# A fused attention and two mixers on one core: third-pass weights from ScalarE's queue, earlier stores, earlier token mixing, another order of Strassen's first products

## The chip, the cores and the metric

The kernel runs on one core of a Trainium2 chip. The metric is the device time of one execution in microseconds; it is the median of three runs. One further execution was profiled, and all durations come from that one.

## The reference

Float32, batch 2, 768 tokens, 8 heads of 64. The middle stage's and the last stage's weights arrive as float64.

```python
def reference(q, k, v, centroids, ...):
    # cluster attention: a key counts only where its cluster is the query's
    mask = argmax(qn @ cn.T) == argmax(kn @ cn.T)
    scores = where(mask, q @ k.T / sqrt(64), -1e9)
    x = (softmax(scores) @ v)                  # -> (2, 768, 512)
    # mixer 1
    u = x + (x.T @ U @ V).T                    # rank 32 over the 768 tokens
    x = u + maximum(u @ w_ch1, 0) @ w_ch2      # 512 -> 2048 -> 512
    # mixer 2
    u = x + (maximum(x.T @ w_tok1, 0) @ w_tok2).T   # 768 -> 256 -> 768
    return u + maximum(u @ w_ch1, 0) @ w_ch2   # 512 -> 1536 -> 512
```

## The kernel before

Each operand of a matrix product is held as a high and a low part, so that each product is three matmuls (high·high, high·low, low·high). There are three stages on one core.

**Attention** fills the first 239 us or so, and isn't touched.

**Mixer 1's channel mixing** takes the 1536 tokens in three passes of 512 over the 16 blocks of weights, which makes 48 units. A unit is two *half slots*: `hidden(k+1)`, 12 matmuls of 512 columns into one PSUM bank, and `outmm(k)`, 12 matmuls that accumulate into four banks. `hidden_out` turns a hidden bank into the operand of `outmm`: ScalarE takes the Relu (L786), and VectorE then the low part (L787), each from PSUM. The half slots are numbered 0 to 95. The first two passes keep their weights in SBUF; those of the third come back from DRAM (`scr_a`) by `feed`, 32 loads of 512 KB into three buffers. At half slot n, `feed(n)` may issue one load: a unit's first half once `hidden_out` of the unit two ahead of it is written into the program, its second half once the `outmm` two units ahead is. Either load has then three half slots until its first use.

Beside this runs work in the background, a piece each half slot. `conv_rest` turns mixer 2's float64 weights into high and low parts, a *quad* of blocks at a time: a raw load of 1 MB (L535), ScalarE's L96, VectorE's L100, L103, L106 and L109, sums of blocks for Strassen's scheme (step 6), the high parts on ScalarE and GpSimd's low parts (step 7), VectorE's low part (step 7.5), and two stores into `scr_b` of 768 KB and 1 MB (step 8, L617 and L618). A table, `line`, gives each quad a half slot h, and the steps stand at fixed distances from it. `tok(0)`, the token mixing of the first batch, begins at half slot 68 and goes in 20 pieces: 6 of transposes, 6 of the first product and 8 of the second. Behind it, `build_u(0)` makes the operands of Strassen's products out of the result, 18 small operations, three in a half slot, on ScalarE, VectorE and GpSimd.

**Mixer 2's channel mixing** is Strassen's scheme: seven products for each pair of blocks. Six *runs* of 14 steps follow one another. In a step TensorE does six matmuls of 384 columns of a hidden product for the next run (`h_mm`) and six of an output product of this run (`o_mm`). Then `h_out` works the hidden product off, and `o_out` (VectorE, L1150) adds the output product to the result, in this order on VectorE. `CHAIN` lets products alternate between two banks; the bank of the last output product, steps 12 and 13, is the one with which the next run begins. `ORDER` lists the seven products in the order in which both kinds are made; `CHUNKS` and `PLACE` say which of them one load brings and where they lie in `scr_b`. `tok(1)` and the first run's hidden products stand ahead of the runs, `build_u(1)` beside the first two.

SP issues all the DMAs of the second and third stage, in program order: an issue that waits holds all that stand behind it. The loads' and stores' completions are counted on eight semaphores, in turn.

Of the kernel before, what the change touches and what calls it, by code (L numbers as in the profile page):

```python
# [24 lines left out]
def tile_cluster_attention__then__two_mixers(  # L25
# [895 lines left out]
    def rest_of_u():  # L921
# [21 lines left out]
        for i in range(len(ops) + 1):  # L943
# [13 lines left out]
            (wide, 13, 37), (wide, 14, 40), (wide, 15, 43), (mixer, 1, 46), (mixer, 2, 48), (mixer, 3, 50)]  # L957
    line += [(quad, q, h) for q, h in enumerate((54, 59, 62, 65, 69, 72, 75, 79, 82, 85, 89, 92))]
    for n, (f, k, h) in enumerate(line, 6):
        steps = [(h - 4, (3,)), (h - 3, (4, 4.5)), (h - 2, (5, 5.5))]  # L960
        if f is quad:
            steps += [(h - 1, (6,)), (h, (7,)), (h + 1, (7.5,)), (h + 3, (8,))]
        else:
            steps += [(h, (6, 6.5)), (h + 1, (7,))]
        if n > 7:
            steps.append((line[n - 8][2] - 1, (1,)))
        for s, ds in steps:
            for d in ds:
                at(wides, s, (f, k, d, n))
# [6 lines left out]

    ORDER = (1, 5, 6, 3, 7, 2, 4)
    PLACE = (0, 3, 4, 5, 6, 1, 2)
# [5 lines left out]
    FRESH = (True, True, False, False, False, True, False)  # L984

    slot = lambda x, i: x[:, 1536 * i : 1536 * i + 1536].rearrange("p (h c n) -> p h c n", h=2, c=2)
    pos = lambda i: ORDER.index(i)
    base = [slot(u1_, i) for i in range(3)] + [slot(wx_, i) for i in range(2)] + [slot(qk_, 7), slot(vz, 0)]
# [3 lines left out]
    def build_u(b):  # L992

        B = {(i, j): x2[b][:, 2 * i : 2 * i + 2, ts(j, HS)] for i in range(2) for j in range(2)}
        o = {i: ops_u[b][pos(i)] for i in ORDER}
        hi = lambda i: o[i][:, 0]
        lo = lambda i: o[i][:, 1]

        def flat(i, x):
            return [lambda: rnd(act, hi(i), x), lambda: sub(pool, lo(i), x, f32(hi(i)))]  # L1000

        t = [fz[:, 768 * i : 768 * i + 768].rearrange("p (c n) -> p c n", c=2) for i in range(2)]

        def cut(i, x, eng=pool):
            return [lambda: rnd(act, hi(i), x), lambda: sub(eng, lo(i), x, f32(hi(i)))]

        def add(o, x, y, op):
            return [lambda: dve.tensor_tensor(out=o, in0=x, in1=y, op=op)]  # L1008

        return (flat(1, B[0, 0]) + add(t[0], B[0, 0], B[0, 1], ALU.subtract) + cut(5, t[0], dve) + add(t[1], B[1, 1], t[0], ALU.add)  # L1010
                + cut(6, t[1], dve) + add(t[0], B[1, 0], t[1], ALU.subtract) + flat(3, B[1, 1])
                + add(t[1], B[1, 1], B[0, 1], ALU.subtract) + cut(7, t[1]) + flat(2, B[1, 0]) + cut(4, t[0], dve))

    gfree = [x.rearrange("p (h n) -> p h n", h=2) for x in (qk_[:, ts(i, 2 * HS)] for i in range(14))]
    gs = {}
    tmps, w1b = [], []
# [22 lines left out]
    def load1(n):  # L1039
        if n < len(seq1):  # L1040
            b, pr, c = seq1[n]
            s, m = CHUNKS[c]
            x = w1b[n % len(w1b)][:, 0 : 512 * m]
            sp.dma_start(f32(x), scr2[pr, 0, :, 512 * PLACE[s] : 512 * (PLACE[s] + m)])
            for i in range(m):
                at1[b, pr, s + i] = x[:, ts(i, 512)].rearrange("p (h n) -> p h n", h=2), n, i == m - 1

    def load2(n):
        if n < len(seq2):
            b, k, c = seq2[n]  # L1050
            s, m = CHUNKS[c]
            x = w2b[n % len(w2b)][:, 0 : 1024 * m].rearrange("p (r n) -> p r n", r=2)
            sp.dma_start(f32(x), scr2[2 * k : 2 * k + 2, 1, :, 512 * PLACE[s] : 512 * (PLACE[s] + m)].rearrange("r p n -> p r n"))
            for i in range(m):
                at2[b, k, s + i] = x[:, :, ts(i, 512)].rearrange("p r (h n) -> p r h n", h=2), n, i == m - 1

# [3 lines left out]
    def h_mm(b, pr, s):  # L1060
        w, n, ends = at1[b, pr, s]
        u = ops_u[b][s]
        o, on = ps[:, HB[pr % 2][CHAIN[s]], 0:HS], dict(skip_group_check=not FRESH[s])
        for c in range(2):
            cs = ts(c, P)
            mm(o, w[:, 0, cs], u[:, 0, c, :], c == 0 and FRESH[s], False, **on)
            mm(o, w[:, 0, cs], u[:, 1, c, :], False, False, **on)
            mm(o, w[:, 1, cs], u[:, 0, c, :], False, c == 1, **on)
        if ends:
            load1(n + len(w1b))  # L1070

    def h_out(b, pr, s):
# [17 lines left out]

        if s == 0:
            held_[1] = tmp()
            act.copy(held_[1], x)
        elif s == 1:
            held_[3] = tmp()
            act.copy(held_[3], x)
        elif s == 2:
            held_[0] = tmp()
            act.copy(held_[0], x)
        elif s == 3:  # L1100
            dve.tensor_tensor(out=held_[0], in0=x, in1=held_[0], op=ALU.add)
            act.activation(held_[0], held_[0], AF.Relu)
        elif s == 4:
            new(3, 7)
            held_[7] = tmp()
            dve.tensor_tensor(out=held_[3], in0=x, in1=held_[3], op=ALU.add)
            top(3, held_[3])
            relu_less(held_[7], held_[3], held_[0], ALU.subtract)
            cut(7, held_[7])
        elif s == 5:  # L1110
            new(1, 5, 6)
            held_[5], held_[6] = tmp(), tmp()
            dve.tensor_tensor(out=held_[1], in0=x, in1=held_[1], op=ALU.add)
            top(1, held_[1])
            relu_less(held_[5], held_[1], held_[0], ALU.subtract)
            cut(5, held_[5])
            relu_less(held_[6], held_[3], held_[5], ALU.add)
            rnd(act, hi(6), held_[6])
            low(1, held_[1])
            low(3, held_[3])  # L1120
        else:
            new(2, 4)
            top(2, x)
            relu_less(held_[0], x, held_[6], ALU.subtract)
            sub(pool, lo(6), held_[6], f32(hi(6)))
            cut(4, held_[0])
            low(2, x)

    def o_mm(b, k, s, j):
        w, n, ends = at2[b, k, s]  # L1130
        o, on = ps[:, OB2[j][CHAIN[s]], 0:HS], dict(skip_group_check=not FRESH[s])
# [28 lines left out]
    bg = [rest_of_u(), conv_rest()]  # L1160
    while done < 68:
        for t in bg:
# [34 lines left out]
    for r, (b, k) in enumerate(runs):  # L1197
# [3 lines left out]
        for i in range(14):  # L1201
# [6 lines left out]
            if nxt:  # L1208
                for x in {6: (), 7: (6, 7)}.get(i, (i,)):
                    h_out(nxt[0], 2 * nxt[1] + x // 7, x % 7)  # L1210
            o_out(b, k, s_, j)
            send(2 if nxt else 0)
# [45 lines left out]
```

## Time and profile before

| | us |
|---|---|
| three runs | 758.09, 756.66, 754.59 |
| median | 756.66 |
| the profiled execution | 757.82 |
| its span | 756.0 |
| TensorE matmuls, busy | 730.5 (97%) |
| VectorE, busy | 565.1 (75%) |
| ScalarE, busy | 371.9 (49%) |
| GpSimd, busy | 221.9 (29%) |
| DMA, moved | 165.36 MB, 219 GB/s on average |

Busy is what an engine's instructions cover of the span. A matmul that runs at half the clock counts as busy too, so that a busy TensorE may still lose time. All times in the rows are from the start of the span.

### The profile page before, as it was taken

To read this page: it belongs to the slowest core of one execution; us is meant where nothing else is said; L and a number is where in the kernel's file an instruction comes from. 1 tells how busy PE (TensorE), PEld (TensorE's weight loads), DVE (VectorE), ACT (ScalarE), POOL (GpSimd) and SP (SyncE) were. 2 spreads that over 40 slices of the span, in tenths; PEclk is the share of its full clock that TensorE was granted. 3 is DMA by queue.
4 is the path that set the end of the run, shared out by engine and by line. 5 is a ranking of instruction groups with operands and counts; after the bars stand their busy time and mean duration, and the time that the engine had idled before them with its cause. 6 is when DMAs were issued, how large, how long until landed. Compare 5 with 4: busy or idle time off the path is not lost.

```text
span 756.0 us, 11118 instructions
## 1 busy us (share of the span) xinstructions
PE 730.5 (97%) x4046; PEld 606.9 (80%) x4046; DVE 565.1 (75%) x829; ACT 371.9 (49%) x660; POOL 221.9 (29%) x181
## 2 busy tenths in 40 slices
PE   7899999999999999999999899999699999899998
PEld 6676777776776888888888677888589999899997
DVE  7778898877875658867878886789855687675674
ACT  7678778777785533333334334333243435333330
POOL 6233153133111123341332212122521425242230
PEclk9999999999999999999999999999899999999999
DMA  6797588765231446763536799989745877587734
GB/s 180 188 226 206 148 218 217 198 186 122 66 102 67 156 178 231 270 222 134 201 114 234 300 410 359 394 309 413 250 151 171 337 258 248 173 292 266 260 132 160
DMA packets 54134, 165.36 MB, mean 219 GB/s; under 512 B 7456, under 2 KB 16544, under 8 KB 50496
## 3 DMA queue, kind: packets, MB, share of 16 engines
q1 hardware_dynamic: 53648, 163.83, 65.4%
q10 hardware_dynamic: 432, 0.82, 0.3%
q8 instruction: 32, 0.52, 0.3%
q14 instruction: 22, 0.18, 0.1%
HBM read 103.61 MB, written 41.94 MB: 193 GB/s over the span
## 4 chain that ended last, share of the span: by engine, by line
PE 85%; DVE 8%; DMA 5%; issue 1%; ACT 1%; POOL 0%; SPq 0%; POOLq 0%; DVEq 0%; ACTq 0%
PE ps L73 74%; PE ps L323 9%; DMA qk<-scr_a 2%; DMA scr_b<-qk 1%; DMA tt<-scr_b 1%; DVE mid L1058 1%; PE ps L386 1%; PE ps L343 1%; DVE qk L1058 1%; DVE fz L1008 1%; DVE c__78 L109 1%; PE ps L409 0%; DMA qk<-p 0%; DVE fz L85 0%; DVE ug L85 0%
## 5 line engine op out<-in xcount | busy, mean ns | idle before, releaser
L73 PE MATMUL ps<-ug,qk 128*128 128x512 f32 x576 | 143.7, 402 | 10.4 <-DVE ug L787 5.7
L73 PEld LDWEIGHTS ps<-ug,qk 128*128 128x128 f32 x576 | 111.0, 194 | 34.8 <-DVE ug L787 6.4
L73 PE MATMUL ps<-qk 112*128 112x384 f32 (+2 forms) x480 | 114.7, 366 | 3.5 <-DMA qk<-p 2.0
L73 PE MATMUL ps<-qk,tt 128*128 128x384 f32 (+1 forms) x528 | 107.9, 344 | 4.4 <-DVE xn L1150 4.1
L301 DVE TENSOR_REDUCE nm<-ps 128x1 f32<-128x768 f32 x96 | 91.2, 955 | 27.9 <-PE ps L73 26.6
L73 PEld LDWEIGHTS ps<-qk,tt 128*128 128x128 f32 x528 | 94.6, 189 | 7.9 <-DVE xn L1150 6.4
L306 ACT ACTIVATE p<-ps,nm 128x768 f32<-128x768 f32 x96 | 86.2, 900 | 22.5 <-DVE nm L301 21.8
L323 PEld LDWEIGHTS ps<-ident,p 128*128 128x128 f32 x576 | 68.4, 141 | 32.6 <-issue 26.9
L323 PE MATMUL ps<-ident,p 128*128 128x128 f32 x576 | 91.0, 278 | 0.5 <-DVE pt L328 0.3
L73 PEld LDWEIGHTS ps<-qk 112*128 112x128 f32 (+1 forms) x480 | 80.7, 190 | 12.4 <-issue 4.4
L786 ACT ACTIVATE ug<-ps 128x512 fp32r<-128x512 f32 x48 | 28.6, 596 | 114.7 <-PE ps L73 109.8
L1150 DVE TENSOR_TENSOR xn<-ps,xn 128x384 f32<-128x384 f32 x84 | 46.0, 553 | 39.0 <-PE ps L73 38.8
L787 DVE SCALAR_TENSOR_TENSOR ug<-ps,ug 128x512 fp32r<-128x512 f32 x48 | 33.1, 689 | 54.1 <-ACT ug L786 54.0
L85 POOL TENSOR_TENSOR qk<-mid,qk 128x384 fp32r<-128x384 f32 x36 | 41.5, 1161 | 107.8 <-ACT qk L78 94.5
L73 PE MATMUL ps<-pt,vr 128*64 128x384 f32 x384 | 72.1, 498 | 0.0
L85 POOL TENSOR_TENSOR qk<-c__78,qk 128x512 fp32r<-128x512 f32 (+1 forms) x26 | 33.9, 1323 | 128.1 <-ACT qk L78 111.8
L330 ACT COPY pt<-ps 128x512 f32<-128x512 f32 x96 | 55.7, 586 | 25.1 <-PE ps L323 24.0
L73 PEld LDWEIGHTS ps<-pt,vr 128*64 128x64 f32 x384 | 23.5, 136 | 25.8 <-issue 25.4
L106 DVE SCALAR_TENSOR_TENSOR c__78<-c__77,c__78 128x1024 int32<-128x1024 int32 (+2 forms) x32 | 42.9, 1341 | 0.2
L85 POOL TENSOR_TENSOR am<-am,amx 128x384 f32<-128x384 f32 (+1 forms) x13 | 10.9, 841 | 109.1 <-DVE amx L214 74.6
L109 DVE SCALAR_TENSOR_TENSOR c__78<-c__77,c__78 128x1024 int32<-128x1024 int32 (+2 forms) x32 | 41.6, 1299 | 1.0
L96 ACT ACTIVATE c__78<-c__77 128x1024 f32<-128x1024 f32 (+2 forms) x32 | 35.5, 1110 | 12.5 <-DMA c__77<-in_wb_dram 6.0
(216 smaller groups left out, 1215.2 us busy)
## 6 DMA issues: line engine op xcount, KB each, us to landing
tt<-scr_b SPq DMA_DIRECT2D x18, 1024.0 KB, 6.3
c__77<-in_wa_dram SPq DMA_DIRECT2D x16, 1024.0 KB, 4.9
qk<-scr_a SPq DMA_DIRECT2D x32, 512.0 KB, 12.8
ring<-scr_b SPq DMA_DIRECT2D x30, 512.0 KB, 4.9
c__77<-in_wb_dram SPq DMA_DIRECT2D x12, 1024.0 KB, 7.7
scr_b<-qk SPq DMA_DIRECT2D x12, 1024.0 KB, 13.0
scr_a<-qk SPq DMA_DIRECT2D x16, 512.0 KB, 2.8
scr_a<-wx SPq DMA_DIRECT2D x12, 512.0 KB, 3.5
```

Of the source, the lines that this page charges most:

```text
L73: pe.matmul(o, lhsT=l, rhs=r, start=start, stop=stop, **kw)
L85: eng.tensor_tensor(out=o, in0=a, in1=b, op=ALU.subtract)
L96: act.activation(dst, hi.bitcast(F32), AF.Abs)
L106: dve.scalar_tensor_tensor(out=d, in0=lo, scalar=29, in1=d, op0=ALU.logical_shift_right, op1=ALU.bitwise_or)
L109: dve.scalar_tensor_tensor(out=d, in0=hi, scalar=-0x40000000, in1=d, op0=ALU.bitwise_and, op1=ALU.bitwise_or)
L301: dve.tensor_reduce(out=nm[:, n % 4 : n % 4 + 1], in_=ps[:, b0 : b0 + 2, 0:HS], axis=AX.XY, op=ALU.max, negate=True)
L306: act.activation(p32[n % NP32].rearrange("p (j k) -> p j k", j=2), ps[:, b0 : b0 + 2, 0:HS], AF.Exp, bias=nm[:, n % 4 : n % 4 + 1], accum_ ...
L323: pe.transpose(ps[:, tb[j], ts(i, P)], p32[n % NP32][:, ts(c, P)], ident)
L330: act.copy(o, ps[:, tb[j], :])
L786: act.activation(gh, o, AF.Relu)
L787: dve.scalar_tensor_tensor(out=gl, in0=o, scalar=0.0, in1=f32(gh), op0=ALU.max, op1=ALU.subtract)
L1150: dve.tensor_tensor(out=o, in0=ps[:, OB2[j][CHAIN[s]], 0:HS], in1=o, op=ALU.add)
```

## The change

Four edits, here with the lines that the argument needs. `feed` issues its loads on ScalarE's queue in place of SP's. The quads come up to two half slots earlier from the fifth on, and each is stored two half slots behind its h in place of three. `tok(0)` begins at half slot 66 in place of 68, and with it all that follows it. Strassen's hidden products get an order of their own, `HORDER`; products 1 and 3 are now finished early, and the cuts of products 4 and 7 are put off to the first step of the next pair.

```diff
-                sp.dma_start(f32(weights(u)[:, i, :, :]).rearrange("p h n -> p (h n)"), scr[f, i])
+                act.dma_start(f32(weights(u)[:, i, :, :]).rearrange("p h n -> p (h n)"), scr[f, i])
...
-    line += [(quad, q, h) for q, h in enumerate((54, 59, 62, 65, 69, 72, 75, 79, 82, 85, 89, 92))]
+    line += [(quad, q, h) for q, h in enumerate((54, 59, 62, 65, 68, 71, 75, 78, 81, 84, 87, 90))]
-            steps += [(h - 1, (6,)), (h, (7,)), (h + 1, (7.5,)), (h + 3, (8,))]
+            steps += [(h - 1, (6,)), (h, (7,)), (h + 1, (7.5,)), (h + 2, (8,))]
...
-    ORDER = (1, 5, 6, 3, 7, 2, 4)
-    CHUNKS = ((0, 1), (1, 2), (3, 2), (5, 2))
+    HORDER, ORDER = (1, 2, 6, 5, 7, 3, 4), (1, 5, 6, 3, 7, 2, 4)
+    HCHUNKS, CHUNKS = ((1, 2), (6, 5), (7, 3), (4,)), ((1,), (5, 6), (3, 7), (2, 4))
...
+    def flush():
+        while behind:
+            behind.pop(0)()
...
         if s == 0:
+            flush()
             held_[1] = tmp()
             act.copy(held_[1], x)
         elif s == 1:
-            held_[3] = tmp()
-            act.copy(held_[3], x)
+            new(1)
+            dve.tensor_tensor(out=held_[1], in0=x, in1=held_[1], op=ALU.add)
+            top(1, held_[1])
+            low(1, held_[1])
...
         elif s == 3:
+            held_[3] = tmp()
+            act.copy(held_[3], x)
+        elif s == 4:
+            new(3)
+            dve.tensor_tensor(out=held_[3], in0=x, in1=held_[3], op=ALU.add)
+            top(3, held_[3])
+            low(3, held_[3])
+        elif s == 5:
+            new(5, 6)
+            held_[5], held_[6] = tmp(), tmp()
             dve.tensor_tensor(out=held_[0], in0=x, in1=held_[0], op=ALU.add)
             act.activation(held_[0], held_[0], AF.Relu)
...
-            new(1, 5, 6)
-            held_[5], held_[6] = tmp(), tmp()
-            dve.tensor_tensor(out=held_[1], in0=x, in1=held_[1], op=ALU.add)
-            top(1, held_[1])
             relu_less(held_[5], held_[1], held_[0], ALU.subtract)
             cut(5, held_[5])
             relu_less(held_[6], held_[3], held_[5], ALU.add)
-            rnd(act, hi(6), held_[6])
-            low(1, held_[1])
-            low(3, held_[3])
+            cut(6, held_[6])
         else:
-            new(2, 4)
+            new(2, 4, 7)
             top(2, x)
-            relu_less(held_[0], x, held_[6], ALU.subtract)
-            sub(pool, lo(6), held_[6], f32(hi(6)))
-            cut(4, held_[0])
             low(2, x)
+            relu_less(held_[1], x, held_[6], ALU.subtract)
+            relu_less(held_[5], held_[3], held_[0], ALU.subtract)
+            behind.extend([lambda h=held_[5], c=cut: c(7, h), lambda h=held_[1], c=cut: c(4, h)])
...
-    while done < 68:
+    while done < 66:
```

**First place: where the third pass begins.** These are rows of SP's queue before. `c__77` is the raw weights' buffer, `qk` and `vz` hold the weights' buffers and the converted operands.

```order
L535 DMA c__77<-in_wb_dram 128x2x512
L766 DMA qk<-scr_a 128x1024
L535 DMA c__77<-in_wb_dram 128x2x512
L766 DMA qk<-scr_a 128x1024
L617 DMA scr_b<-qk 128x1536
L618 DMA scr_b<-qk 128x2048
L766 DMA qk<-scr_a 128x1024 x2
L535 DMA c__77<-in_wb_dram 128x2x512
L766 DMA qk<-scr_a 128x1024
```

A load of weights (L766) stands behind raw loads and stores there. These are ScalarE's rows of the changed kernel at the same place; the Relu is L786, and L879 is a copy of `tok(0)`.

```order
L786 ACTIVATE ug<-ps 128x512
L766 DMA qk<-scr_a 128x1024
L879 CAST wx<-ps 128x512
L766 DMA qk<-scr_a 128x1024
L879 CAST wx<-ps 128x512
L96 ACTIVATE c__78<-c__77 128x1024
L786 ACTIVATE ug<-ps 128x512
L766 DMA qk<-scr_a 128x1024
```

The loads have left SP's queue, where only L535, L617 and L618 remain, and stand among ScalarE's own work.

**Second place: VectorE late in the third pass.** These are the rows between two low parts of the hidden bank (L787) before; `fz` is scratch, L1008 a sum of `build_u(0)`, L85 a low part or a difference.

```order
L787 SCALAR_TENSOR_TENSOR ug<-ps,ug 128x512
L85 TENSOR_TENSOR qk<-fz,qk 128x4x256
L106 SCALAR_TENSOR_TENSOR c__78<-c__77,c__78 128x1024
L109 SCALAR_TENSOR_TENSOR c__78<-c__77,c__78 128x1024
L85 TENSOR_TENSOR u_2310<-fz,u_2310 128x768
L1008 TENSOR_TENSOR fz<-xn,fz 128x768
L85 TENSOR_TENSOR fz<-c__78 128x256
L85 TENSOR_TENSOR fz<-c__78,fz 128x256 x2
L607 SCALAR_TENSOR_TENSOR fz<-c__78 128x256
L1008 TENSOR_TENSOR fz<-xn 128x768
L787 SCALAR_TENSOR_TENSOR ug<-ps,ug 128x512
```

These are the rows between the same two low parts in the changed kernel, where the sums of `build_u(0)` are L1003.

```order
L787 SCALAR_TENSOR_TENSOR ug<-ps,ug 128x512
L85 TENSOR_TENSOR qk<-fz,qk 128x4x256
L106 SCALAR_TENSOR_TENSOR c__78<-c__77,c__78 128x1024
L109 SCALAR_TENSOR_TENSOR c__78<-c__77,c__78 128x1024
L85 TENSOR_TENSOR u_2310<-fz,u_2310 128x768
L1003 TENSOR_TENSOR fz<-xn,fz 128x768
L85 TENSOR_TENSOR fz<-c__78 128x256
L85 TENSOR_TENSOR fz<-c__78,fz 128x256 x2
L607 SCALAR_TENSOR_TENSOR fz<-c__78 128x256
L85 TENSOR_TENSOR wx<-fz,wx 128x768
L1003 TENSOR_TENSOR fz<-xn 128x768
L787 SCALAR_TENSOR_TENSOR ug<-ps,ug 128x512
```

Between these two low parts stands the same work with one more difference, `wx<-fz,wx`, which stood ahead of the first of them before. What moved is what stands behind: two hidden units' low parts in place of one follow the last sums.

**Third place: VectorE at the end of a run.** These are its rows before, at steps 12 and 13, where L1113 works off the bank of step 12's hidden product, L1058 are the sums with a Relu that follow, and L1150 adds step 12's output product.

```order
L1113 TENSOR_TENSOR mid<-ps,mid 128x384
L1058 SCALAR_TENSOR_TENSOR mid<-mid,fz 128x384
L1058 SCALAR_TENSOR_TENSOR mid<-fz,mid 128x384
L1058 SCALAR_TENSOR_TENSOR qk<-mid,qk 128x384
L1058 SCALAR_TENSOR_TENSOR qk<-fz,qk 128x384
L1150 TENSOR_TENSOR xn<-ps,xn 128x384
```

These are the rows of the changed kernel there, with L1118 for L1113 and L1153 for L1150.

```order
L1118 TENSOR_TENSOR mid<-ps,mid 128x384
L1058 SCALAR_TENSOR_TENSOR mid<-mid 128x384 x2
L1153 TENSOR_TENSOR xn<-ps,xn 128x384
```

Two of the five instructions ahead of the output's sum have moved, to steps 1 and 4 of the pair.

## Rows read from the trace of the kernel before

**Rows 1.** The page, part 4: shares of the chain that ended last.

```profile
PE 85%; DVE 8%; DMA 5%; issue 1%; ACT 1%; POOL 0%; SPq 0%; POOLq 0%; DVEq 0%; ACTq 0%
```

**Rows 2.** TensorE's waits over the span: us in total, times, longest.

```profile
PE ps L73 <- DVE ug L787: 5.7, 1, 5.7
PE ps L73 <- DVE xn L1150: 4.1, 4, 2.5
...
PE ps L73 <- DMA qk<-scr_a: 2.1, 2, 2.0
```

**Rows 3.** TensorE's timeline: start, duration, instructions.

```profile
423.87 2.88 PE L73 MATMUL ps<-ug,wx 128*128 128x512 f32 x12
426.59 2.88 PE L73 MATMUL ps<-ug,qk 128*128 128x512 f32 x12
...
463.80 2.88 PE L73 MATMUL ps<-ug,qk 128*128 128x512 f32 x12
...
467.88 2.88 PE L73 MATMUL ps<-ug,qk 128*128 128x512 f32 x12
```

**Rows 4.** Stretches: us, busy of PE, PEld, DVE, ACT, POOL, PEclk, DMA, GB/s.

```profile
429.32:432.02 2.70, 0.16 (x1) 0.03 (x1) 1.76 (x6) 1.05 (x2) 1.44 (x2) 0.96 1.02 419
432.02:439.05 7.03, 7.03 (x25) 5.65 (x26) 5.39 (x6) 1.50 (x3) 0.00 (x0) 0.77 1.02 418
...
454.81:459.23 4.42, 4.42 (x12) 3.42 (x13) 3.84 (x4) 2.53 (x5) 2.43 (x2) 0.61 1.01 386
```

**Rows 5.** Stretches at the end of the third pass, columns as in group 4.

```profile
514.77:547.42 32.65, 26.92 (x109) 21.63 (x109) 29.64 (x31) 12.32 (x18) 15.34 (x8) 0.90 0.83 318
533.80:540.05 6.25, 0.52 (x4) 0.10 (x2) 6.18 (x9) 2.26 (x4) 2.86 (x2) 0.80 0.51 206
540.05:547.42 7.37, 7.37 (x23) 5.92 (x24) 5.30 (x6) 2.24 (x4) 4.90 (x2) 0.70 0.75 251
```

**Rows 6.** Stretches of the third stage, columns as in group 4.

```profile
547.42:556.39 8.97, 8.46 (x55) 7.46 (x53) 4.68 (x9) 5.13 (x10) 0.00 (x0) 1.00 0.70 261
...
646.79:650.54 3.75, 3.75 (x12) 3.75 (x13) 2.76 (x5) 0.89 (x2) 1.00 (x1) 0.54 0.56 231
```

**Rows 7.** The issue of a third-pass load at 420.4 us: KB, us to landing.

```profile
qk<-scr_a SPq DMA_DIRECT2D x1, 512.0 KB, 11.5
```

**Rows 8.** The chain that ended last, near 440 us: start, duration, what.

```profile
438.01 1.24 DVE c__78 L109
...
439.77 14.90 DMA qk<-scr_a
```

**Rows 9.** DMA from 415 to 540 us; KB each, median us to landing.

```profile
DMA packets 9672, 43.88 MB, mean 351 GB/s; under 512 B 960, under 2 KB 960, under 8 KB 8384
...
qk<-scr_a SPq DMA_DIRECT2D x31, 512.0 KB, 12.9
scr_b<-qk SPq DMA_DIRECT2D x10, 1024.0 KB, 13.2
```

**Rows 10.** DMA queues from 2 to 6 us (q1 SP's, q10 ScalarE's): packets, MB, share.

```profile
q1 hardware_dynamic: 253, 0.66, 54.2%
q10 hardware_dynamic: 259, 0.53, 37.7%
```

**Rows 11.** The page, part 6: the quickest transfer of half a megabyte, us to landing.

```profile
scr_a<-qk SPq DMA_DIRECT2D x16, 512.0 KB, 2.8
```

**Rows 12.** ScalarE's timeline near 530 us: start, duration, instruction.

```profile
529.46 0.58 ACT L786 ACTIVATE ug<-ps 128x512 fp32r<-128x512 f32 x1
```

**Rows 13.** VectorE's timeline from 530 to 540 us, columns as in group 12.

```profile
530.84 2.75 DVE L109 SCALAR_TENSOR_TENSOR c__78<-c__77,c__78 128x1024 int32<-128x1024 int32 x1
...
539.30 0.69 DVE L787 SCALAR_TENSOR_TENSOR ug<-ps,ug 128x512 fp32r<-128x512 f32 x1
```

**Rows 14.** VectorE's timeline at the last change of runs, columns as in group 12.

```profile
733.24 0.56 DVE L1113 TENSOR_TENSOR mid<-ps,mid 128x384 f32<-128x384 f32 x1 [0.39 <-PE ps L73]
...
736.78 0.54 DVE L1150 TENSOR_TENSOR xn<-ps,xn 128x384 f32<-128x384 f32 x1
```

More of the change, by code (lines that the diff above doesn't have):

```diff
@@ L995, in build_u, with cut @@
         o = {i: ops_u[b][pos(i)] for i in ORDER}
[L996 to L1000, printed above, removed]
         t = [fz[:, 768 * i : 768 * i + 768].rearrange("p (c n) -> p c n", c=2) for i in range(2)]
-        def cut(i, x, eng=pool):
-            return [lambda: rnd(act, hi(i), x), lambda: sub(eng, lo(i), x, f32(hi(i)))]
+        def cut(i, x, eng):
+            hi, lo = o[i][:, 0], o[i][:, 1]
+            return [lambda: rnd(act, hi, x), lambda: sub(eng, lo, x, f32(hi))]
         def add(o, x, y, op):
             return [lambda: dve.tensor_tensor(out=o, in0=x, in1=y, op=op)]
-        return (flat(1, B[0, 0]) + add(t[0], B[0, 0], B[0, 1], ALU.subtract) + cut(5, t[0], dve) + add(t[1], B[1, 1], t[0], ALU.add)
-                + cut(6, t[1], dve) + add(t[0], B[1, 0], t[1], ALU.subtract) + flat(3, B[1, 1])
-                + add(t[1], B[1, 1], B[0, 1], ALU.subtract) + cut(7, t[1]) + flat(2, B[1, 0]) + cut(4, t[0], dve))
+        early, last = cut(4, t[1], dve), []
+        if b == 0:
+            early, last = last, early
+        return (cut(1, B[0, 0], pool) + cut(2, B[1, 0], pool) + add(t[0], B[0, 0], B[0, 1], ALU.subtract)
+                + add(t[1], B[1, 1], t[0], ALU.add) + cut(6, t[1], dve) + add(t[1], B[1, 0], t[1], ALU.subtract) + early
+                + cut(5, t[0], dve) + add(t[0], B[1, 1], B[0, 1], ALU.subtract) + cut(7, t[0], pool) + cut(3, B[1, 1], pool) + last)
     gfree = [x.rearrange("p (h n) -> p h n", h=2) for x in (qk_[:, ts(i, 2 * HS)] for i in range(14))]
-    gs = {}
+    gs, behind = {}, []
     tmps, w1b = [], []
@@ L1041, in load1 @@
             b, pr, c = seq1[n]
-            s, m = CHUNKS[c]
+            ch = HCHUNKS[c]
+            m, s0 = len(ch), min(STORED.index(i) for i in ch)
             x = w1b[n % len(w1b)][:, 0 : 512 * m]
-            sp.dma_start(f32(x), scr2[pr, 0, :, 512 * PLACE[s] : 512 * (PLACE[s] + m)])
-            for i in range(m):
-                at1[b, pr, s + i] = x[:, ts(i, 512)].rearrange("p (h n) -> p h n", h=2), n, i == m - 1
+            sp.dma_start(f32(x), scr2[pr, 0, :, 512 * s0 : 512 * (s0 + m)])
+            for i in ch:
+                at1[b, pr, i] = x[:, ts(STORED.index(i) - s0, 512)].rearrange("p (h n) -> p h n", h=2), n, i == ch[-1]
     def load2(n):
@@ L1050, in load2 @@
             b, k, c = seq2[n]
-            s, m = CHUNKS[c]
+            ch = CHUNKS[c]
+            m, s0 = len(ch), min(STORED.index(i) for i in ch)
             x = w2b[n % len(w2b)][:, 0 : 1024 * m].rearrange("p (r n) -> p r n", r=2)
-            sp.dma_start(f32(x), scr2[2 * k : 2 * k + 2, 1, :, 512 * PLACE[s] : 512 * (PLACE[s] + m)].rearrange("r p n -> p r n"))
-            for i in range(m):
-                at2[b, k, s + i] = x[:, :, ts(i, 512)].rearrange("p r (h n) -> p r h n", h=2), n, i == m - 1
+            sp.dma_start(f32(x), scr2[2 * k : 2 * k + 2, 1, :, 512 * s0 : 512 * (s0 + m)].rearrange("r p n -> p r n"))
+            for i in ch:
+                at2[b, k, i] = x[:, :, ts(STORED.index(i) - s0, 512)].rearrange("p r (h n) -> p r h n", h=2), n, i == ch[-1]
     def relu_less(o, x, y, op):
@@ L1060, in h_mm @@
     def h_mm(b, pr, s):
-        w, n, ends = at1[b, pr, s]
+        w, n, ends = at1[b, pr, HORDER[s]]
         u = ops_u[b][s]
-        o, on = ps[:, HB[pr % 2][CHAIN[s]], 0:HS], dict(skip_group_check=not FRESH[s])
+        o, on = ps[:, HB[pr % 2][CHAIN[s]], 0:HS], dict(skip_group_check=not HFRESH[s])
         for c in range(2):
             cs = ts(c, P)
-            mm(o, w[:, 0, cs], u[:, 0, c, :], c == 0 and FRESH[s], False, **on)
+            mm(o, w[:, 0, cs], u[:, 0, c, :], c == 0 and HFRESH[s], False, **on)
             mm(o, w[:, 0, cs], u[:, 1, c, :], False, False, **on)
@@ L1210, in tile_cluster_attention__then__two_mixers @@
                     h_out(nxt[0], 2 * nxt[1] + x // 7, x % 7)
+            if not nxt:
+                flush()
             o_out(b, k, s_, j)
```

16 lines of the change are left out of this document (4 added, 12 removed).

## Prediction

> **What bounds the kernel now.** I first read the chain that ended last: 85% of it is TensorE, 8% VectorE, 5% DMA [rows 1]. So the end comes sooner only where TensorE stops waiting or runs faster; no matmul is removed by this change. I then listed TensorE's waits [rows 2]. Three belong to stages that the change touches: 5.7 us once for the low part of a hidden bank (VectorE, L787), 4.1 us in four pieces for an output sum (L1150), 2.1 us for loads of weights. Last I cut the span into stretches around each, with the granted clock beside the busy time. There the reader is to see that a wait costs twice. Twelve matmuls take 2.72 us from start to start [rows 3], so 24 take 5.44; behind the wait that ends at 432.02 the same 24 take 7.03 at a mean clock of 0.77, and behind that at 454.81 twelve take 4.42 at 0.61 [rows 4]. So the engine goes down towards its lower level (1.2 of 2.4 GHz) after it stood still.
>
> The losses, each with its clock:
>
> - **A**, 429.32 to 432.02: the next matmuls start 2.70 us late (the 0.16 busy in it is the end of those before), and 7.03 − 5.44 = 1.59. Sum 4.3.
> - **C**, before 454.81: 2.0 idle [rows 2], and 4.42 − 2.72 = 1.70. Sum 3.7.
> - **E**, 533.80 to 540.05: 6.25 − 0.52 = 5.73 idle, and 7.37 − 5.44 = 1.93 [rows 5]. Sum 7.7.
> - **Changes of runs** in the third stage: 4.1 idle [rows 2]; and behind the longest, 646.79 to 650.54, twelve matmuls of 384 columns take 3.75 us [rows 6] where 2.72 · 384/512 = 2.04 is due, which is 1.7. Sum 5.8.
>
> **The loads on ScalarE's queue (A and C).** Both waits are for loads that came late. That of 420.4 us took 11.5 to land [rows 7], at 431.9, just as TensorE started again. That of C stood on SP behind a raw load that waited for VectorE's L109 (done at 439.25), was issued at 439.77 and took 14.90 [rows 8]. The median load of this stage takes 12.9 us, and the stores in the same queue 13.2 [rows 9], while the DMA engines are full (a share of 1.02 at 418 GB/s [rows 4]). Half a megabyte at 418 GB/s is 1.25 us of that; the rest is standing in line.
>
> On a queue of its own a load needn't stand behind 1.75 MB of stores. Where two queues had work at the same time, at the start of the kernel, they moved 253 and 259 packets, 0.66 and 0.53 MB [rows 10]: about half each. At half of 418 GB/s a load takes 2.5 us, two in a row 5; the quickest transfer of that size lands in 2.8 [rows 11], 1.5 more than its 1.25. So I estimate 4 to 6.5 us to landing. What is there in time? ScalarE issues a unit's first half only behind the Relu of the unit two ahead, three half slots before its use: 3 · 2.72 = 8.2 us, less about 1 for the Relu (0.58 [rows 12]) and the issue, so 7.2. With a piece of token mixing's products in each half slot, which then takes 463.80 to 467.88 = 4.08 [rows 3], it is 11. So I take A and C as gone, −4.3 and −3.7; the bounds are all of it and nothing. The margin in half slots without token mixing is thin.
>
> The 32 issues stand among ScalarE's own work now; ScalarE is busy 12.3 of 32.7 us in the densest stretch [rows 5], where the time to issue hides. What is queued behind an issue that waits (for the semaphore of the eighth DMA before it, often a store) is the next Relu, and behind that VectorE's L787 and `outmm`. The Relu is wanted only two half slots later, 5.4 us, of which Relu and low part need 1.3: some 4 us of cover.
>
> The Trainium skill speaks against this edit. Its page "DMA: Bandwidth & Descriptors", section "Issuing engines are not separate DMA queues", says that DMAs started by several engines run on the same 16 DMA engines and interleave, and that starting them on several saves only the sequencer's time to issue. By that rule alone A and C stay, and the sum would be 754.0. The same page's section "Queues, rings and completion order" says that each DMA engine takes turns between the queues, packet by packet; the trace agrees with that one by its 253 and 259 packets.
>
> **Earlier stores, earlier token mixing.** They remove nothing. The bytes stay (43.88 MB from 415 to 540 us, 351 GB/s on average [rows 9]); a quad's stores come a half slot sooner or more, and some raw loads too, so the line of waiting bytes near 430 us rather grows. That costs nothing as long as the loads have their own turn; if they haven't, it is rival 3. `tok(0)`'s matmuls only change places with half slots that had none. I set both at 0.
>
> **E stays.** ScalarE had the high part ready at 529.46 + 0.58; VectorE made the low part only at 539.30 [rows 12, 13]. VectorE was busy 29.64 of 32.65 us [rows 5], partly because its instructions are stretched where GpSimd works: L109 takes 2.75 us at 530.84 [rows 13] and 1.24 at 438.01 [rows 8]. In the changed order the work between these two low parts is the same and one difference more (about 1 us), which stood just ahead before. The two half slots won behind `build_u(0)` lie behind the stall and can't shorten it. What A and C give back doesn't make it longer either, since VectorE's line of work is paced by the half slots until 514 us. So 0, with bounds −7.7 (rival 2) and +1.
>
> **Changes of runs.** The bank of step 12 is that of the next run's step 0. VectorE's sum for it stood behind L1113 and four more instructions: from 733.24 to 736.78 + 0.54 is 4.1 us [rows 14]. At the last change of runs three groups of six matmuls lie between, 3.06 us, at the others four; so TensorE waits by about 1 there, and elsewhere where `build_u(1)` and GpSimd slow VectorE. Now three instructions stand ahead of it, an add and two sums (0.56 each, as L1113), but between them a Relu on ScalarE that VectorE waits for (at most 0.58, as the wider one [rows 12]). So 3 · 0.56 + 0.58 + 0.54 = 2.8 us, and some 0.1 to 0.2 for handing over: just under 3.06. I take the 5.8 as gone. Bounds: nothing of it, or all.
>
> The new order's costs: at step 1 of each pair VectorE has an add and a low part more (1.1 us). During the runs a step of 2.04 us has room for it; but beside `tok(1)`, 547.42 to 556.39, where TensorE stands for 0.5 already [rows 6], half of it may show: +0.5, bounds 0 and 1.1. The two cuts that `flush` puts ahead of the copy at the next pair's first step are two ScalarE instructions, 1.1 us by the Relu's row, and with the copy 1.6, inside a step of 2.04: nothing, with 0.4 us of cover.
>
> **What else.** `build_u(1)` still puts GpSimd beside VectorE at the first changes of runs, whose longest wait of 2.5 [rows 2] with its clock (4.2 in all) could partly stay: I take 1.0, bounds 0 and 4.2. ScalarE's issues that wait, and a load that lands a little late: 0.5, bounds 0 and 2.
>
> **Sum**, against the profiled execution: 757.8 − 4.3 − 3.7 − 5.8 + 0.5 + 1.0 + 0.5 = 746.0. The median of the runs lies 1.2 under that execution (756.66 against 757.82), so 744.8; I say **745**. The forecast's own range is 742 (none of the additions at all) to 750 (what else at 5 us in place of 1.5, and the 1.1).
>
> **The rivals.**
>
> 1. *The loads come no sooner.* A line of bytes in front of full engines is as long whoever issues, if the load is served in the order of issue: A and C stay, 745 + 8 = 753. The Trainium skill's rule on issuing engines, above, says as much. For it: the engines are full, and the total is unchanged. Against it: the weights need 0.5 MB per half slot of 2.72 us, 193 GB/s, which is less than half of 418, and the two queues at the start shared evenly.
> 2. *E goes too.* If the light half slots let VectorE catch up sooner than I see: 745 − 7.7 = 737. Against it: the same instructions in the same order, at the second place above.
> 3. *Slower: ScalarE issues too late.* SP could issue a load as soon as its buffer was free, up to five half slots ahead; ScalarE can only behind a Relu, three ahead. If a load still takes the 12.9 us of now, the half slots of the full stretch (415 to 459 us, some 12) last (12.9 + 1)/3 = 4.6 in place of 2.72, 23 us more, of which 8 are there already. Half of the other 15, since the line of stores gets shorter while TensorE waits, is 7.5 on a kernel that keeps its other gains: 745 + 8 + 7.5 = 761. It decides from the point where a load takes over 7.2 us from issue to landing in half slots without token mixing. For it: nearly every load takes longer than that now. Against it: half of the packets would do for 6.5.
> 4. *Strassen's new order opens waits.* `flush` and the round trip to the Relu have covers of 0.4 and 0.1 us. If VectorE or ScalarE is later than that in each run, the 5.8 aren't saved: 751, and up to 756 with a lower clock behind each of the waits.
>
> **How the numbers follow.** The forecast has 0.55, rival 1 0.10, rival 2 0.11, rival 3 0.10, rival 4 0.14. 0.5% of 756.7 is 3.8 us, about what a measurement of this kernel can tell from no change: faster is below 752.9, slower above 760.4. The forecast and rival 2 are faster (0.66), of rival 4 two thirds (0.10), of rival 1 less than half (0.04): 0.80. Slower is rival 3 but for a little: 0.09. The rest is 0.11. For 8 in 10 the range goes from the upper half of rival 2 to rival 4's end, 738 to 756, which leaves out about 0.06 below and 0.10 above.
>
> **What would show it.** Right: no wait of TensorE for a load from 415 to 460 us, and loads on ScalarE's queue that land in under 8 us; one wait of some 6 us for L787 near 530; no wait over 0.5 us for an output sum, save at the first changes of runs. Wrong in the loads: landing 10 us or more after the issue, TensorE waiting for one after another, a clock under 0.9 over the whole stretch. Wrong in E: no wait for L787. Wrong in the third stage: TensorE waiting for VectorE's sums at other steps than a run's first, or for ScalarE's copies at step 7.

## The result

The changed kernel takes 749.25 us at the median (748.31 to 749.93, 4 runs) against 755.96 of the kernel before (4 runs): a ratio of 0.9912, 95% interval 0.9886 to 0.9939. It is faster, by 6.7 us where 11 were forecast; the time lies inside the range of 738 to 756, near the upper end of the forecast's own. The profiled execution took 749.86 us, 8.0 less than that of before.

TensorE's waits over the span, in the changed kernel (us in total, times, longest):

```profile
PE ps L73 <- DVE ug L787: 6.2, 2, 5.2
PE ps L73 <- DVE xn L1153: 2.1, 4, 1.2
...
PE ps L73 <- ACT mid L1098: 0.8, 1, 0.8
PE ps L73 <- DMA tt<-scr_b: 0.8, 1, 0.8
PE ps L73 <- issue: 0.7, 1, 0.7
```

Beside [rows 2] the reader sees: no wait for a load of the third pass is left; the long wait for L787 stays (5.2 us in place of 5.7), and a second one of 1.0 has come; the waits for output sums are halved, not gone; two waits of 0.8 us stand in the third stage, a new one for ScalarE's copy of a hidden bank (L1098, L1093 before) and one for a load (0.2 before); and one of 0.7, at 431.30 us, has no releaser that the trace names ("issue").

The stretches between the same matmuls in the two traces, by TensorE's timeline: the third pass from its twelve matmuls `ps<-u,tt` (404.83 before, 405.54 after) to the first `ps<-u,ring` (547.42, 541.52) went from 142.6 to 136.0 us, −6.6. From there to the first output product (583.70, 577.68) 36.3 and 36.2. The runs, from there to the last matmul's end (752.59, 744.03), 168.9 and 166.4, −2.5. What lies ahead of all this, untouched, took 0.7 more in this execution. These three stretches are used below: *third pass* and *runs* are meant in this sense.

### The profile page after: what moved, and what is told of

Read it like the earlier page. It is cut to its first block, busy times and chain, and to the rows that moved or that the text cites. A ratio compares the mean times of both kernels' runs of the same rounds, so it can differ in the third digit from the quotient of the medians.

```text
span 747.6 us, 11096 instructions
## 1 busy us (share of the span) xinstructions
PE 728.4 (97%) x4046; PEld 604.8 (81%) x4046; DVE 557.6 (75%) x829; ACT 370.5 (50%) x660; POOL 215.1 (29%) x181
## 4 chain that ended last, share of the span: by engine, by line
PE 81%; DVE 10%; DMA 3%; ACT 2%; issue 2%; POOL 1%; SPq 0%; ACTq 0%; DVEq 0%; POOLq 0%
PE ps L73 70%; PE ps L323 9%; DVE mid L1058 1%; DVE fz L85 1%; DVE qk L1058 1%; DMA pt<-in_qT_dram 1%; DVE qk L85 1%; DMA tt<-scr_b 1%; DVE xn L1153 1%; PE ps L343 1%; PE ps L386 1%; DVE c__78 L106 1%; DMA scr_b<-qk 1%; DVE ug L787 1%; PE ps L409 1%
## 5 line engine op out<-in xcount | busy, mean ns | idle before, releaser
L73 PE MATMUL ps<-ug,qk 128*128 128x512 f32 x576 | 140.5, 396 | 6.9 <-DVE ug L787 6.2
L73 PEld LDWEIGHTS ps<-ug,qk 128*128 128x128 f32 x576 | 108.8, 190 | 30.2 <-DVE ug L787 7.0
L786 ACT ACTIVATE ug<-ps 128x512 fp32r<-128x512 f32 x48 | 28.6, 596 | 108.7 <-PE ps L73 103.8
L787 DVE SCALAR_TENSOR_TENSOR ug<-ps,ug 128x512 fp32r<-128x512 f32 x48 | 33.0, 688 | 50.4 <-ACT ug L786 50.3
L85 POOL TENSOR_TENSOR qk<-c__78,qk 128x512 fp32r<-128x512 f32 (+1 forms) x26 | 34.4, 1342 | 120.1 <-ACT qk L78 78.2
L1153 DVE TENSOR_TENSOR xn<-ps,xn 128x384 f32<-128x384 f32 x84 | 46.0, 553 | 27.3 <-PE ps L73 27.1
L85 POOL TENSOR_TENSOR qk<-mid,qk 128x384 fp32r<-128x384 f32 x35 | 35.1, 1020 | 106.6 <-ACT qk L78 103.4
L106 DVE SCALAR_TENSOR_TENSOR c__78<-c__77,c__78 128x1024 int32<-128x1024 int32 (+2 forms) x32 | 42.8, 1337 | 0.2
L85 POOL TENSOR_TENSOR am<-am,amx 128x384 f32<-128x384 f32 (+1 forms) x13 | 10.9, 842 | 109.8 <-DVE amx L214 75.4
L73 PE MATMUL ps<-ug,wx 128*128 128x512 f32 (+1 forms) x180 | 41.9, 379 | 0.0
```

Source lines behind the costliest of these rows:

```text
L73: pe.matmul(o, lhsT=l, rhs=r, start=start, stop=stop, **kw)
L85: eng.tensor_tensor(out=o, in0=a, in1=b, op=ALU.subtract)
L106: dve.scalar_tensor_tensor(out=d, in0=lo, scalar=29, in1=d, op0=ALU.logical_shift_right, op1=ALU.bitwise_or)
L786: act.activation(gh, o, AF.Relu)
L787: dve.scalar_tensor_tensor(out=gl, in0=o, scalar=0.0, in1=f32(gh), op0=ALU.max, op1=ALU.subtract)
L1153: dve.tensor_tensor(out=o, in0=ps[:, OB2[j][CHAIN[s]], 0:HS], in1=o, op=ALU.add)
```

## The experiments

**Each edit alone, and the changed kernel without the queue.** The first four kernels split the change along its edits. First the loads alone (e1):

```diff
-                sp.dma_start(f32(weights(u)[:, i, :, :])...
+                act.dma_start(f32(weights(u)[:, i, :, :])...
```

> The kernel before with one edit: the third pass's loads are issued on ScalarE's queue. Theory: both waits for loads and their low clock go (4.3 and 3.7 us), the stall for L787 near 534 us stays at 5 to 7 us, the third stage is as before: about 748 us, 8 less than before. Rival: the loads only come in time because the quads' stores and token mixing also moved; then this edit alone gives less than 4 us, and TensorE still waits for a load near 430 or 453 us.

Measured: ratio 0.9984 (0.9971 to 0.9997), 755.58 us beside 756.45. The rival has it: some 1.2 us, and TensorE still waits for loads, 0.73, 0.83 and 0.79 us at 426.74, 430.61 and 443.94. Why, ScalarE's timeline of this kernel shows (rows with ACTq are DMA issues; in brackets idle time and what ended it):

```profile
423.41 0.96 ACTq L766 DMA_DIRECT2D qk<-scr_a  x2
427.46 0.94 ACT L78 ACTIVATE qk<-c__78 128x256 fp32r<-128x256 f32 x2 [3.47 <-DMA scr_b<-qk]
431.30 1.06 ACT L78 ACTIVATE qk<-fz 128x1024 fp32r<-128x1024 f32 x1 [2.90 <-DMA scr_b<-qk]
431.50 0.84 ACTq L766 DMA_DIRECT2D qk<-scr_a  x2
```

Two conversions of a quad wait until a store has left their buffer, and the next two loads, at 431.50, stand behind them on ScalarE: 8 us after the last ones. And a load doesn't get half of the bytes. These are the two queues of this kernel from 424 to 430 us (packets, MB, share):

```profile
q1 hardware_dynamic: 251, 1.64, 64.9%
q10 hardware_dynamic: 252, 0.90, 36.7%
```

As many packets, but SP's are larger. 0.90 MB in 6 us is 150 GB/s, where a load every 2.72 us needs 193. The loads' median to landing was 9.0 us.

The schedule alone (e2; both lines of the diff on the quads, and `while done < 66`):

> The kernel before with the earlier quads, the earlier stores and token mixing from half slot 66, and the loads still on SP's queue, Strassen's order as before. Theory: nothing gained, and the stores that come earlier stand ahead of the loads in the same queue: 755 to 759 us, with TensorE still waiting 2 us or more for loads between 420 and 460 us. Rival: the schedule is what brings the gain of the third pass; then about 749.

Measured: 0.9962 (0.9947 to 0.9978), 752.72 us. My theory is refuted: the schedule, for which I had forecast nothing, gives more than the queue, though the intervals overlap a little and the rival's 749 isn't reached. With the loads still on SP, 0.68 us is left of the wait near 430 us, put down to no load; one of 1.74 for a load stays at 449.89.

Strassen's order alone (e3):

> The kernel before with the new order of Strassen's hidden products alone. Theory: what the runs of the third stage give in the changed kernel, 2.5 us from the first output product to the end, comes from this edit alone: about 753.5 us. Rival: it was a gift of the other edits (stores and loads out of the way), then within 1 us of before.

Measured: 0.9978 (0.9968 to 0.9989), 754.52 us; the runs take 166.3 us as in the changed kernel, the third pass waits for its loads as before (2.52 and 2.18). As the theory has it, if with a little less.

This trace also tells what the prediction's wait A is for. The kernel before has it put down to a conversion of a quad (L78); here the same matmuls wait for the load. First the kernel before, then this one:

```profile
432.02 7.18 PE L73 MATMUL ps<-ug,qk 128*128 128x512 f32 x24 [2.54 <-ACT qk L78]
```

```profile
432.45 7.32 PE L73 MATMUL ps<-ug,qk 128*128 128x512 f32 x24 [2.52 <-DMA qk<-scr_a]
```

The changed kernel without the queue (e4):

```diff
-                act.dma_start(f32(weights(u)[:, i, :, :])...
+                sp.dma_start(f32(weights(u)[:, i, :, :])...
```

> The changed kernel with the third pass's loads put back on SP's queue. Theory: the waits for loads come back, 6 to 8 us, so 755 to 757 us, TensorE waiting for loads between 420 and 460 us. Rival: with the new schedule SP's queue would do as well, 749 to 751.

Measured: 0.9943 (0.9929 to 0.9957), 751.73 us, between the two. Waits of 0.37 and 1.90 us for loads come back. So beside the schedule the queue is worth some 0.3%, 2.4 us, by two intervals that overlap (0.9929 to 0.9957 here, 0.9886 to 0.9939 with the queue).

**Which part of the schedule.** The new theory came from SP's timeline. In the kernel before, a quad's stores go out like this:

```profile
418.17 0.38 SPq L535 DMA_DIRECT2D c__77<-in_wb_dram  x1
...
419.11 0.42 SPq L617 DMA_DIRECT2D scr_b<-qk  x1
419.58 0.74 SPq L618 DMA_DIRECT2D scr_b<-qk  x1
```

A step at h + 3 stands behind the next raw load in SP's program, and that one waits for its buffer, until VectorE's L109. One kernel stores at h + 2 and changes nothing else (f1):

```diff
-            steps += [..., (h + 3, (8,))]
+            steps += [..., (h + 2, (8,))]
```

> The kernel before with one edit: each quad is stored two half slots behind its h, not three. Theory (formed on the schedule's run): a store at three half slots stands on SP behind the next quad's raw load, which waits for its buffer, and so goes out 3 to 6 us late and in a bunch with the loads of weights; at two half slots it stands ahead of that raw load and uses time in which the DMA engines are idle. Then this edit alone takes the wait near 430 us away (the stores go out near 413 and 416 us, not 419), about 3 to 4 us: 752 to 753. Rival: the token mixing that starts two half slots sooner is what gives the loads time; then 756.

Measured: 0.9947 (0.9926 to 0.9967), 751.95 us. One digit gives 4 us, as much as the schedule as a whole (the intervals overlap). In its trace the third pass takes 136.5 us, against 136.0 with all four edits, and two shorter waits are left in place of 2.54, 0.17 and 1.97:

```profile
430.39 5.76 PE L73 MATMUL ps<-ug,qk 128*128 128x512 f32 x24 [1.11 <-issue]
437.51 2.97 PE L73 MATMUL ps<-ug,qk 128*128 128x512 f32 x12 [0.93 <-DMA qk<-scr_a]
```

SP's timeline of this kernel has the stores ahead of the raw load, 7.3 and 4.0 us sooner, both more than the half slot of 2.72 by which the step moved:

```profile
411.82 0.32 SPq L617 DMA_DIRECT2D scr_b<-qk  x1
415.59 0.32 SPq L618 DMA_DIRECT2D scr_b<-qk  x1
417.93 0.38 SPq L535 DMA_DIRECT2D c__77<-in_wb_dram  x1
```

And the bytes go where there was room. The stretch from 412 to 418 us, first of the kernel before, then of this one (the last three columns are the clock, the DMA engines' share and GB/s):

```profile
412.00:418.00 6.00, 6.00 (x29) 4.95 (x28) 5.65 (x7) 2.57 (x3) 0.00 (x0) 1.00 0.26 105
```

```profile
412.00:418.00 6.00, 6.00 (x28) 4.96 (x27) 5.62 (x8) 2.57 (x3) 0.00 (x0) 1.00 0.83 339
```

The engines were a quarter busy just ahead of the jam. Another thing changed with it, and no run separates the two: ScalarE's conversions no longer wait for a store (6.2 us in three waits from 405 to 535 us before, none here).

The wait of 1.11 us that is left has another cause, as far as the traces show. GpSimd's low parts, which such a conversion held until 428.80 in the kernel before, start at 426.63 here, beside two differences of VectorE (L85); these take 2.27 us in place of 0.89, and the last sums of the second pass (L804) stand behind them. The matmuls go on 0.85 us after these sums begin. No run tests this.

Mixing alone (f2):

```diff
-    while done < 68:
+    while done < 66:
```

> The kernel before with one edit: token mixing of the first batch from half slot 66. Theory of the stores: it only lengthens two half slots by the transposes and gives nothing, 755 to 757, with the waits near 430 and 453 us as before. Rival: half slots with token mixing in them last longer than those without, so that loads have more time; then 752 to 753.

Measured: 1.0083 (1.0064 to 1.0102), 762.5 us, outside of what both said. In this kernel `build_u(0)` writes its last operand into `vz` ahead of the store of a quad that lies there, so that one quad's weights aren't the reference's. SP's own waits show what that does to the time:

```profile
SPq L617 <- DVE vz L85: 21.2, 1, 21.2
```

The store waits 21.2 us for `build_u(0)`, with the third pass's last load behind it, and TensorE then waits 2.83 us for a load at 549.78. So this run doesn't price the mixing alone. It shows that mixing at 66 can't stand without the earlier quads or the earlier stores; which of the two it needs, it doesn't show.

The clean test leaves mixing and places as before, with the queue, the stores and Strassen's order of the change (g2):

```diff
-    line += [(quad, q, h) for q, h in enumerate((54, 59, 62, 65, 68, 71, 75, 78, 81, 84, 87, 90))]
+    line += [(quad, q, h) for q, h in enumerate((54, 59, 62, 65, 69, 72, 75, 79, 82, 85, 89, 92))]
...
-    while done < 66:
+    while done < 68:
```

> The kernel before with the loads on ScalarE's queue, the stores at two half slots, and Strassen's new order, but the quads' places and the start of token mixing (68) as before. Theory: the stores alone gave 4.2 us, Strassen's order 1.9; the earlier places and the earlier mixing give nothing or cost 1 to 2 us, and the queue has little left to give: 747.5 to 749.5, the changed kernel's time or less. Rival: the earlier mixing and places are worth what the schedule and the queue gain together; then 750.5 or more.

Measured: 0.9914 (0.9899 to 0.9929), 749.75 us: the changed kernel's ratio, and just above the theory's 749.5. Beside the other edits the earlier mixing and places are worth nothing that can be told.

**Is it the packets?** The queue's edit with stores of half the width (f3):

```diff
-            sp.dma_start(scr2[pr, w, :, 0:1536], f32(A)...
-            sp.dma_start(scr2[pr, w, :, 1536:3584], f32(B)...
+            for o, t, m in ((0, A, 1536), (1536, B, 2048)):
+                x = f32(t).rearrange("p i h n -> p (i h n)")
+                for j in range(0, m, m // 2):
+                    sp.dma_start(scr2[pr, w, :, o + j : o + j + m // 2], x[:, j : j + m // 2])
```

> The kernel before with the loads on ScalarE's queue and each of a quad's two stores cut into two halves of its columns, so that a store's rows are 3 and 4 KB, not 6 and 8; the bytes are the same. Theory: two queues take turns packet by packet, SP's packets are larger, and so ScalarE's queue gets 36% of the bytes where both have work (0.90 of 2.54 MB from 424 to 430 us), 150 GB/s where the weights need 193. With smaller packets on SP its share goes to 45% or more while stores run, the loads land in under 8 us at the median (9.0 with the queue alone), and the time is 1 to 3 us less than with the queue alone: 753 to 754.5. Rival: the loads come late since ScalarE issues them late; then landing and time stay as with the queue alone, 755.5, or get worse through the two more DMAs of each quad.

Measured: 0.9985 (0.9972 to 0.9998), 755.12 us; no gain over the queue alone. The queues from 424 to 430 us:

```profile
q10 hardware_dynamic: 376, 1.34, 54.9%
q1 hardware_dynamic: 377, 1.17, 47.9%
```

The theory of the share holds: packet for packet, and the bytes go with the packet's size. The loads land in 7.7 us at the median. But it doesn't make the kernel faster. ScalarE now waits for stores (10.2 us in three waits for L78, from 405 to 535 us, where the queue alone had 6.4 in two), and the loads are issued late behind that. That speaks for the rival: with late stores, the loads' lateness on ScalarE is in their issue. What the two more DMAs of each quad cost isn't priced apart.

**The stall for L787.** In the changed kernel, `build_u(0)` from half slot 90 (f4):

```diff
-        for _ in range(3):
+        for _ in range(3 if done >= 90 else 0):
             if todo:
                 todo.pop(0)()
```

> The changed kernel, with the 18 operations of the first batch's operands for Strassen's products begun at half slot 90, not at 86, still three in a half slot. Theory: the stall for L787 near 529 us is VectorE's line of work, in which four sums and two differences of these (0.95 us each alone, up to 1.4 beside GpSimd) stand ahead of the low part; behind half slot 92 VectorE has 4 us idle. With them moved there the waits for L787 (6.2 us and their low clock) fall to under 1.5 us: 742 to 744. Rival: VectorE is late by the quads' work alone, or the operands are now late for the first hidden products of the third stage; then a wait of the same size stands there, 748 to 750.

Measured: 0.9864 (0.9842 to 0.9886), 745.82 us, above the theory's 742 to 744. No wait for L787 is left in its trace, but a new one stands before the last twelve matmuls of the third pass. TensorE's, ScalarE's and SP's timelines of this kernel:

```profile
532.20 4.37 PE L73 MATMUL ps<-ug,qk 128*128 128x512 f32 x12 [2.82 <-ACT vz L78]
```

```profile
525.02 0.85 ACT L78 ACTIVATE u<-fz 128x768 fp32r<-128x768 f32 x1 [3.57 <-DVE fz L1003]
525.08 0.33 ACTq L766 DMA_DIRECT2D qk<-scr_a  x1
```

```profile
520.35 4.37 SPq L1043 DMA_DIRECT2D ring<-scr_b  x4
```

These matmuls don't read `vz`. What they need and what was late is the last load: issued at 525.08, it landed 7.0 us later, at 532.1. It was held on ScalarE behind a conversion that waited 3.57 us for VectorE, with four loads of the third stage already out. That is rival 3 of the prediction, at one place. The test that decides between this reading and the trace's own gives the last two units' loads back to SP (g1):

```diff
-                act.dma_start(f32(weights(u)[:, i, :, :])...
+                (act if u < K - 2 else sp).dma_start(f32(weights(u)[:, i, :, :])...
```

> The changed kernel with the 18 operations from half slot 90, and the last two units' loads of the third pass issued by SP again. Theory: the wait of 2.8 us before the last twelve matmuls of the third pass, which the late build had, is for the last load: ScalarE issued it at 525.1 us behind an operation of the build that waited for VectorE, and it landed behind four loads of the third stage. From SP it goes out ahead of these; the wait and its low clock (1.5 us) go, 741.5 to 743. Rival: the trace's own reading, a wait for ScalarE's part of product 4; then the wait stays and the time is as with the late build, 745.8.

Measured: 0.9811 (0.9796 to 0.9827), 742.14 us. The wait is gone, 0.85 us for L787 has come up, and the third pass takes 128.8 us against 136.0 in the changed kernel.

**The change of runs.** VectorE's timeline of the changed kernel at the last one, and the matmuls that wait:

```profile
728.23 0.56 DVE L1058 SCALAR_TENSOR_TENSOR qk<-ps,qk 128x384 fp32r<-128x384 f32 x1 [0.56 <-ACT qk L1086]
728.71 0.55 DVE L1058 SCALAR_TENSOR_TENSOR mid<-ps,mid 128x384 f32<-128x384 f32 x1
729.17 0.55 DVE L1058 SCALAR_TENSOR_TENSOR mid<-mid 128x384 f32<-128x384 f32 x1
729.63 1.02 DVE L1153 TENSOR_TENSOR xn<-ps,xn 128x384 f32<-128x384 f32 x2
```

```profile
726.76 2.28 PE L73 MATMUL ps<-qk,tt 128*128 128x384 f32 x12
730.24 13.79 PE L73 MATMUL ps<-qk,tt 128*128 128x384 f32 x78 [1.20 <-DVE xn L1153]
```

The twelve matmuls at 726.76 are step 13 and the next run's step 0: these go on without a wait, so step 12's sum is in time, as forecast. Step 1 waits, for step 13's sum, which stands behind the low part and the two sums of the last hidden product. One edit puts it ahead of them (g3, on top of g1):

```diff
+            if i == 13:
+                o_out(b, k, s_, j)
             if nxt:
                 for x in {6: (), 7: (6, 7)}.get(i, (i,)):
                     h_out(nxt[0], 2 * nxt[1] + x // 7, x % 7)
             if not nxt:
                 flush()
-            o_out(b, k, s_, j)
+            if i < 13:
+                o_out(b, k, s_, j)
```

> The kernel g1 with one edit: at the last step of a run VectorE adds the output product ahead of what it does with the hidden product. Theory: at a change of runs TensorE now waits for the bank of step 13, whose sum stands behind three instructions of the last hidden product; ahead of them, the waits for output sums (1.9 to 2.1 us, the last of 1.2) fall under 0.6 us and the time by 1.3 to 2 us against g1. Rival: the sum of step 12, which stands behind a round trip to ScalarE, is as late; then the wait of about 1 us stays.

Measured: 0.9798 (0.9784 to 0.9812), 741.36 us beside 742.14: 0.8 us less, where 1.3 to 2 were expected, and the two intervals overlap. Its waits show that the mechanism holds and where the rest went:

```profile
PE ps L73 <- ACT mid L1098: 1.4, 2, 0.9
...
PE ps L73 <- DVE xn L1153: 0.5, 1, 0.5
```

The waits for sums fell from 2.1 to 0.5, the last one is gone; but a second wait for ScalarE's copy at step 7 has opened. The last edit is about that copy (g4, on top of g3):

```diff
         if s == 0:
-            flush()
             held_[1] = tmp()
             act.copy(held_[1], x)
+            flush()
```

> The kernel g3 with one edit: at the first step of a pair the copy of the hidden bank stands ahead of the two cuts that were put off, not behind. Theory: the wait of 0.85 us at step 7 of the first run is for this copy, held on ScalarE by a cut whose input VectorE made late beside GpSimd; it goes, 0.8 us less than g3. Rival: the cuts are now late for output products 7 and 4, or the sum after the copy is no sooner; then no change.

Measured: 0.9771 (0.9757 to 0.9785), 739.04 us (738.51 to 739.8). No wait for the copy is left, and the runs take 163.0 us (165.2 in g3, 166.4 in the changed kernel). This kernel beats the changed one, which ran in other rounds, by 10 us; between g3 and g4, on the same chip and in the same rounds, it is 2.3 us, with intervals that just touch, where the two waits were 1.4.

## Why the prediction held, and where it didn't

**The loads: right that the waits go, wrong about what takes them away.** I gave A and C, 8.0 us, to ScalarE's queue. Alone it gave 1.2; beside the rest 2.4. Two steps failed. One is "half of 418 GB/s", with 4 to 6.5 us to landing: it was 9.0 with the queue alone and 7.7 in the changed kernel, in part since the queues share packets, not bytes (7.7 too with the queue alone and smaller packets, f3). The other is when a load is issued: ScalarE holds loads behind its own waits. I had looked at that for semaphores and not for the conversions that wait for a store, which put 8 us between two pairs of loads (e1). The signs that I had set for the loads came all the same, no wait for one from 415 to 460 us and a landing under 8 us. But most of the waiting went by the stores: with the loads still on SP, f1 has one wait for a load left, of 0.93 us. As far as the queue goes, the third pass is near its forecast by luck.

The Trainium skill, page "DMA: Bandwidth & Descriptors", section "Issuing engines are not separate DMA queues", says that issuing from several engines saves only the sequencer's time to issue. The 1.2 us of the queue alone are closer to that than to my 8. The same page of the Trainium skill, section "Queues, rings and completion order", has the DMA engines take turns between the queues packet by packet. The runs agree with 251 beside 252 and 377 beside 376 packets.

**The stores: the step that failed most.** "They remove nothing ... I set both at 0", and the line of bytes "rather grows". I looked at the bytes from 415 us on, where the engines are full, and not at the 6 us ahead of it, where they stood at 0.26; and I counted half slots, not what a store stands behind on SP. That it passes the next raw load is what counts: 0.9947 alone, against 0.9984 for the queue, and a third pass of 136.5 us in place of 142.6. For the mixing and the places 0 was right (0.9914 without them).

**E: right.** It stayed, with 6.2 us of waits in place of 5.7, and the cause was the one given, VectorE's line of work in which `build_u(0)` stands ahead of the low part: with that work moved behind it the stall went (f4, g1). The light half slots were there to be used; the change didn't put work into them.

**Changes of runs: the right mechanism, sized at 5.8 less 1.0, measured at 1.7 alone (0.9978) and 2.5 in the runs of the profile.** Step 12's sum is in time as worked out. What I left out is what is late next: step 13's sum, wanted one group of matmuls later, behind three instructions and a Relu. The cover of 0.4 us for `flush` was used up once, and 0.85 more: VectorE's sum for the cut took 1.69 us at 594.68, in place of 0.56, beside GpSimd's `build_u(1)`. So rival 4 came true in part, and the sign "no wait over 0.5 us for an output sum" failed at the last change, with 1.2.

```profile
594.11 1.85 POOL L85 TENSOR_TENSOR ug<-xn,ug 128x768 fp32r<-128x768 f32 x1
594.68 1.69 DVE L1058 SCALAR_TENSOR_TENSOR mid<-fz 128x384 f32<-128x384 f32 x1
```

All waits in the runs together fell by only 0.6 us, from 4.3 to 3.7. The rest of the 2.5 is TensorE's busy time, 164.5 and 162.6 us for the same matmuls: most of it is the low clock behind the longest wait, 0.54 [rows 6], and that part isn't always there. The kernel of e2 has the old order and the same wait, but a clock of 1.00 behind it; its runs take 167.0 us, against 166.3 in the new order. First the kernel before, then e2:

```profile
646.79 2.29 PE L73 MATMUL ps<-qk,tt 128*128 128x384 f32 x6 [2.54 <-DVE xn L1150]
```

```profile
643.08 1.33 PE L73 MATMUL ps<-qk,tt 128*128 128x384 f32 x6 [2.54 <-DVE xn L1150]
```

**The new order's cost beside `tok(1)`** (+0.5 forecast) didn't show: 36.3 and 36.2 us.

**The sum**, forecast at −11.8 against the profiled execution, came out at −8.0: third pass −6.6 (forecast −8.0), runs −2.5 (−4.8), the rest +1.1 (+1.0), 0.7 of it in the stage that isn't touched. Of the 1.4 that the third pass lacks, 0.5 are more waits for L787 and 0.7 the wait at 431.30, where the trace's chain passes VectorE's last sums of the second pass; 0.2 stay without a cause.

## What to carry to other kernels

When a queue is jammed, look at what it did just ahead of the jam: an issue that stands behind another's wait may be most of the cause, and moving it past that wait can give more than a second queue, which only shares the jam (0.9947 and 0.9984 here). A load that moves to a compute engine's queue inherits every wait of that engine's own work. And when a bank's or a buffer's release is made earlier, work out the next one in the same way before counting the gain.

## What the runs showed of the hardware

Two DMA queues with work at the same time take turns by packets, and so the one with the larger packets gets more bytes: 1.64 and 0.90 MB with 251 and 252 packets, 1.17 and 1.34 MB with 377 and 376 when the first one's stores had half the width.

Some of VectorE's instructions took longer while GpSimd worked: the same two differences (L85) 0.89 us with GpSimd idle and 2.27 beside its low parts, a sum of 128x384 0.56 alone and 1.69 beside a low part. All their operands lie in SBUF. The sums with one operand in PSUM (L804) took 2.74 us beside GpSimd in the kernel before, and 2.73 without it in f1.

TensorE's granted clock didn't fall behind every wait of the same length: behind 2.54 us it was 0.54 in the kernel before and 1.00 in e2, at the same matmuls.
